# One maximum instruction for a tile's two heads, and a newly planned order of all steps

## The chip, the cores and the metric

The kernel runs on one core of a Trainium2 chip. The metric is the device time of one execution in microseconds (us). A profile of one further execution was taken by the hardware profiler; the times of single instructions come from it.

## What is computed

Rotary attention followed by a two-layer MLP. q, k and v are float32 arrays of 4 batches, 8 heads, 576 positions and 64 channels.

```python
q_rot, k_rot = (rotate(q), rotate(k))           # by cos and sin of position x frequency
scores = scale * np.matmul(q_rot, k_rot.transpose(0, 1, 3, 2))
scores = scores - np.max(scores, axis=-1, keepdims=True)
attn = np.exp(scores)
attn = attn / (np.sum(attn, axis=-1, keepdims=True) + 1e-09)
attn_out = np.matmul(attn, v)
x = attn_out.transpose(0, 2, 1, 3).reshape(2304, 512)
h = x @ w_in                                    # 512 x 2048
g = np.where(h >= 1, h, np.where(h <= -1, 0.0, (h + 1) ** 2 / 4))
out = g @ w_out                                 # 2048 x 512
```

## The kernel before

**Numbers.** Each float32 operand of a matmul is cut into two 16-bit halves, a high and a low one, and a product is three matmuls (high by high, high by low, low by high; `TERMS`, L601). ACT writes a high half, DVE the low half (`split`, L348). The weights arrive as 64-bit words, are put together from them by three DVE instructions (L506, L508, L510) and are cut in 16 chunks (`prep_w`, L494); for the first ten of them PE and ACT make the low half (L535 to L539), for the rest DVE (L527).

**Attention.** A tile is 128 positions of q for a pair of heads. There are 4 batches x 4 pairs x 4 tiles = 64 of them. `scores` (L573) is one step of 12 matmuls on PE; it fills two PSUM tiles `psS`, one for each head, of two banks each; only the first 576 columns are used. Then `softmax_item` (L548): for each head DVE takes the negative maximum of a row into `mx` (L556), ACT makes the exp with that as its bias and sums the row (L558); ACT scales the sums of both (L561), DVE inverts them (L563), ACT writes each head's high half into `phl` (L566) and DVE its low half (L568). A transpose by the DMA, issued on SP's queue, turns `phl` into `pT` (L300). After two tiles of the same pair of heads comes the step of values, 28 matmuls on PE (`pv_group`, L613, with L611). It uses v in `vS` and copies of it at shifted positions in `vM`, which are written by DMAs on SP's queue (L296, in `prep_v`). The last 64 positions of a batch are left over: for each pair of heads one such tile holds the 64 positions of both heads in its 128 rows, and its softmax has one head's worth of instructions (`attention_left`, L659, with `scores_left`, L588; it uses one of the two `psS` tiles in turn). So there are 2 x 64 + 16 = 144 maxima.

**MLP.** A block of 256 rows of x runs through 8 steps. In each, two groups of 12 matmuls fill `psH` (L692), ACT and DVE form g and its low half (L699 to L713), and two groups of 6 matmuls add to two banks `psO` (L722). ACT writes the result (L732) and SP stores it.

**The order.** Nothing is issued while it is described. Every step is put into a `Plan` (L72) with its engine, its cost in ns, its due time `at`, and what it reads and writes. `wanted` (L113) works out a rank for each step, back from the PE steps in order of `at`; `order` (L132) adds the offsets of the table `SLACK` (L25, in ns, by group and engine and sometimes by part; larger is later) and then simulates five in-order queues, PE, ACT, DVE and the DMA issuers SP and POOL, taking on each the ready step of lowest rank. The steps whose group is `init`, `first` or `raw w` are taken first wherever they are ready. What comes out is the order in which each engine's instructions stand on the chip. The groups have names: `s0` is the softmax of batch 0 and `s1` that of the later batches, `w` the cutting of weights, `k1` the preparing of K for a later batch, `pv` the values, `mlp0` to `mlp3` the blocks of the MLP, and `first` the loads of K, Q and V of batch 0. The costs in question: 760 ns for a scores step (L585), `pe_cost(14, n + 58) + 130` for a values step (L614), which is 2003 ns for n = 256 with `pe_cost` of L279, and for a DMA its bytes at 400 GB/s (L296). `dve_cost` (L285) stands 665 ns for a maximum of 576 columns.

Of the kernel before, what the change touches and what calls it, by code (L numbers as in the profile page):

```python
# [25 lines left out]
    "k0.03 dve": -18_500, "k1 act": 68_700, "k1 dve": 128_000, "k1.12 dve": 2_700, "k1.20 dve": 192_800,  # L26
    "k1.22 act": -86_400, "k1.30 dve": -49_500, "k1.32 act": 53_100, "k1.32 dve": -154_900, "left0 act": 751_500,
    "left0 dve": -109_200, "left0.02 act": -54_200, "left0.03 dve": 207_500, "left1 act": 1_401_000,
    "left1 dve": 2_700, "left1.11 pe": -109_700, "left1.12 act": 41_400, "left1.13 dve": -9_600,
    "left1.30 dve": -29_400, "left1.32 dve": -130_500, "left1.33 pe": 94_600, "mlp0 act": -95_500,  # L30
    "mlp0 dve": -1_118_000, "mlp0 pe": 285_700, "mlp0.0.1 pe": 49_700, "mlp0.0.6 act": -53_100,
    "mlp1 pe": -97_500, "mlp1.1.1 dve": 59_700, "mlp1.1.2 dve": 25_400, "mlp1.1.3 act": 26_000,
    "mlp1.1.5 act": 26_200, "mlp2 act": -133_700, "mlp2 pe": -214_800, "mlp2.2.0 pe": 14_800,
    "mlp2.2.3 act": 167_900, "mlp2.2.3 dve": -287_900, "mlp2.2.3 pe": 44_800, "mlp2.2.7 pe": 97_000,
    "mlp3 act": 8_500, "mlp3 dve": -2_019_800, "mlp3 pe": 139_200, "mlp3.3.0 pe": -130_200,
    "mlp3.3.2 pe": -19_100, "mlp3.3.3 act": -53_700, "mlp3.3.3 pe": -76_300, "mlp3.3.5 act": -184_500,
# [12 lines left out]
    "s0.032 pe": -138_600, "s1 act": 10_000, "s1 dve": 6_000, "s1 pe": -526_500, "s1.100 dve": 8_000,
# [147 lines left out]
def kernel(  # L197
# [12 lines left out]
    nc = tc.nc  # L210
# [12 lines left out]
    def sbt(name, shape, dt=F32):  # L223
        return sb.tile(shape, dt, name=name)
# [661 lines left out]
```

## Time and profile before

| what | value |
|---|---|
| median of 3 runs | 636.36 us (635.49 to 637.52) |
| the profiled execution, its own time | 633.81 us |
| its span, from the first to the last instruction | 632.0 us |
| mean granted TensorE clock | 0.98 of full speed |
| PE busy | 559.8 us, 5078 matmuls |
| DVE busy | 511.2 us, 839 instructions |
| ACT busy | 441.0 us, 881 instructions |
| data moved by the DMA engines | 91.33 MB |

How to read it: PE is TensorE's matmul engine, DVE VectorE, ACT ScalarE, SP and POOL issue DMAs. Each engine works its own queue in order, so an instruction that waits holds up all behind it on that engine. The recorded duration of an instruction on DVE or ACT overlaps the start of the next one a little; the distance from start to start is what it costs the engine. A busy share over the whole span is an average over stages with different limits.

### The profile page before, as it was taken

The page shows a single profiled execution, that of the slowest core. Times are in us where ns is not written, and L with a number is a line of the kernel's source. Part 1 is how long each engine was busy: PE and PEld are TensorE (multiplying, and loading weights), DVE is VectorE, ACT ScalarE, POOL GpSimd, SP SyncE. Part 2 cuts the span into 40 slices and gives each one's busy share as a digit, 9 for nine tenths or more (in the row PEclk, how much of TensorE's full clock was granted, in tenths as well). Part 3 has the DMA queues.
Part 4 walks back from the last instruction along what each step waited for, and adds up shares of the span by engine and source line. Part 5 has one row for each costly group of instructions (what it writes and reads, how often), then busy time and mean ns, then how long its engine had stood idle before and what let it go on. Part 6 is the DMA issues. An engine that isn't in the chain of part 4 may idle for free.

```text
span 632.0 us, 12652 instructions
## 1 busy us (share of the span) xinstructions
PE 559.8 (89%) x5078; PEld 358.6 (57%) x5078; DVE 511.2 (81%) x839; ACT 441.0 (70%) x881; POOL 7.5 (1%) x18
## 2 busy tenths in 40 slices
PE   1346678799997999999998999999999999999995
PEld 1112234566654666666665676676666676666663
DVE  5998999999999999998897889889877874333422
ACT  3647898978999799984878798877787663232221
POOL 0000100000000000000000000000000000000000
PEclk9997879999998999999999999999999999999999
DMA  8997988695699858876377765856666553000000
GB/s 265 372 305 261 258 231 161 133 233 132 142 260 203 195 99 188 205 164 161 92 163 129 124 127 109 136 94 115 113 131 129 85 99 77 1 8 27 1 34 18
DMA packets 188011, 91.33 MB, mean 145 GB/s; under 512 B 170160, under 2 KB 178608, under 8 KB 185904
## 3 DMA queue, kind: packets, MB, share of 16 engines
q1 hardware_dynamic: 186224, 77.94, 56.0%
q0 software_dynamic: 1728, 12.58, 5.6%
q8 instruction: 40, 0.66, 0.4%
q14 instruction: 19, 0.16, 0.1%
HBM read 40.96 MB, written 4.72 MB: 72 GB/s over the span
## 4 chain that ended last, share of the span: by engine, by line
PE 56%; DVE 22%; DMA 12%; ACT 6%; issue 3%; SPq 0%; ACTq 0%
PE psO L722 21%; PE psH L692 21%; PE psV L611 7%; PE psS L582 5%; DMA pT<-phl 5%; DVE phl L568 4%; DVE mx L556 3%; DMA rk<-in_km_dram 3%; DMA vM<-vS 2%; ACT p L558 2%; DVE g L713 1%; ACT phl L566 1%; DMA rv<-in_vm_dram 1%; DVE r L709 1%; DVE xT L508 1%
## 5 line engine op out<-in xcount | busy, mean ns | idle before, releaser
L722 PE MATMUL psO<-w,g 128*128 128x512 f16 x864 | 211.7, 380 | 1.9 <-ACT g L711 0.9
L692 PEld LDWEIGHTS <-w 128*128 128x128 f16 x1920 | 170.9, 98 | 44.4 <-issue 5.2
L692 PE MATMUL psH<-xT,w 128*128 128x256 f16 x1536 | 187.7, 273 | 3.2 <-ACT a L699 3.2
L558 ACT ACTIVATE p<-psS,mx 128x576 f32<-128x576 f32 x144 | 105.3, 733 | 26.1 <-DVE mx L556 20.1
L722 PEld LDWEIGHTS <-g 128*128 128x128 f16 x864 | 79.3, 98 | 75.2 <-DVE g L713 2.5
L568 DVE SCALAR_TENSOR_TENSOR phl<-p,sums,phl 128x576 f16<-128x576 f32 x144 | 113.4, 812 | 9.6 <-ACT phl L566 9.6
L566 ACT ACTIVATE phl<-p,sums 128x576 f16<-128x576 f32 x144 | 105.0, 765 | 17.5 <-DVE sums L563 15.2
L556 DVE TENSOR_REDUCE mx<-psS 128x1 f32<-128x576 f32 x144 | 104.3, 750 | 6.9 <-PE psS L582 6.2
L582 PE MATMUL psS<-kT,qT 64*128 64x512 f16 (+1 forms) x768 | 64.5, 295 | 22.6 <-ACT p L558 15.3
L711 ACT ACTIVATE g<-r 128x512 f16<-128x512 f32 x72 | 44.9, 624 | 47.5 <-DVE r L709 29.2
L699 ACT ACTIVATE a<-psH 128x512 f32<-128x512 f32 x72 | 42.4, 590 | 49.3 <-PE psH L692 48.7
L713 DVE SCALAR_TENSOR_TENSOR g<-r,g 128x512 f16<-128x512 f32 x72 | 49.5, 688 | 26.8 <-ACT g L711 26.7
L582 PEld LDWEIGHTS <-qT 64*128 64x128 f16 x768 | 31.2, 97 | 68.5 <-issue 47.9
L702 DVE SCALAR_TENSOR_TENSOR r<-a 128x512 f32<-128x512 f32 x48 | 33.1, 689 | 45.6 <-ACT a L699 45.2
L611 PE MATMUL psV<-pT,vS 128*64 128x256 f16 (+1 forms) x768 | 50.1, 253 | 3.8 <-DMA pT<-phl 3.5
L709 DVE SCALAR_TENSOR_TENSOR r<-a,r 128x512 f32<-128x512 f32 x72 | 49.6, 689 | 0.9
L611 PEld LDWEIGHTS <-vS 128*64 128x64 f16 x768 | 33.3, 112 | 18.5 <-issue 14.7
L611 PE MATMUL psV<-pT,vM 128*64 128x256 f16 (+1 forms) x480 | 29.2, 253 | 3.3 <-DMA vM<-vS 3.3
L558 ACT ACTIVATION_READ_ACCUMULATOR p<-psS,mx 128x1 f32 x144 | 28.1, 195 | 0.0
L692 PE MATMUL psH<-xL,w 128*128 128x128 f16 x384 | 25.5, 219 | 0.0
L611 PEld LDWEIGHTS <-vM 128*64 128x64 f16 x480 | 22.0, 113 | 4.1 <-DMA vM<-vS 3.8
L535 PE MATMUL psO<-xT,xL 128*128 128x512 f32 x20 | 15.4, 864 | 9.8 <-DVE xT L510 5.6
(98 smaller groups left out, 467.5 us busy)
## 6 DMA issues: line engine op xcount, KB each, us to landing
w<-in_w_in_dram POOLq DMA_DIRECT2D x5, 1024.0 KB, 6.9
rv<-in_vm_dram SPq DMA_DIRECT2D x8, 512.0 KB, 5.7
w<-in_w_out_dram POOLq DMA_DIRECT2D x4, 1024.0 KB, 7.3
out_dram<-o SPq DMA_DIRECT2D x16, 256.0 KB, 2.4
rq<-in_qm_dram SPq DMA_DIRECT2D x7, 512.0 KB, 7.2
dup<-in_qm_dram SPq DMA_DIRECT2D x7, 512.0 KB, 3.9
dup<-in_km_dram SPq DMA_DIRECT2D x6, 576.0 KB, 5.3
rk<-in_km_dram SPq DMA_DIRECT2D x6, 576.0 KB, 6.8
```

What stands on the lines that cost most here:

```text
L556: plan.add("dve", dve_cost(S, psum=True), at, lambda m=m, src=src: nc.vector.tensor_reduce(out=m, in_=src, op=ALU.max, axis=AX.X, negate=T ...
L558: plan.add("act", act_cost(S, psum=True, ptrs=2), at, lambda a=a, e=e, m=m, src=src: nc.scalar.activation(out=p32[e], in_=src, func=AF.Exp ...
L566: plan.add("act", act_cost(S), at, lambda a=a, e=e, hi=hi: nc.scalar.activation(out=hi, in_=p32[e], func=AF.Copy, scale=rr[:, a:a + 1]), r ...
L568: plan.add("dve", dve_cost(S, ptrs=1), at, lambda a=a, e=e, hi=hi, lo=lo: nc.vector.scalar_tensor_tensor(out=lo, in0=p32[e], scalar=rr[:, ...
L582: nc.tensor.matmul(out=psS[a][:, lo:hi], lhsT=qT[hf][d, l, j, c:c + 128], rhs=kT[ks][d, j, m, lo:hi], start=z == 0, stop=z == 2)
L611: nc.tensor.matmul(out=outs[a], lhsT=st, rhs=moving(a, blk), start=z == 0, stop=z == len(seq) - 1)
L692: nc.tensor.matmul(out=psH[:, n * i:n * i + n], lhsT=wi[ft // 2][:, wl, kk, 128 * (ft % 2):128 * (ft % 2) + 128], rhs=xfn(xl, kk), start=z ...
L699: plan.add("act", act_cost(512, psum=True, ptrs=0), at, lambda one=one: nc.scalar.activation(out=a, in_=psH, func=AF.Relu, scale=2.0 ** -7 ...
L709: plan.add("dve", dve_cost(512), at, lambda one=one: nc.vector.scalar_tensor_tensor(out=r, in0=a, scalar=one, in1=r, op0=ALU.max, op1=ALU. ...
L711: plan.add("act", act_cost(512, ptrs=0), at, lambda g=g, one=one: nc.scalar.activation(out=g[:, 0], in_=r, func=AF.Relu, scale=1.0, bias=- ...
L713: plan.add("dve", dve_cost(512), at, lambda g=g, one=one: nc.vector.scalar_tensor_tensor(out=g[:, 1], in0=r, scalar=-one, in1=g[:, 0], op0 ...
L722: nc.tensor.matmul(out=psO[pos[tt]], lhsT=g[:, gl, n * i + 128 * tt:n * i + 128 * tt + 128], rhs=wo[ft // 2][:, wl, ft % 2, :], start=ft = ...
```

## The change

Four things are changed.

- The maxima. For a tile of two heads there is one reduction, which reads 2 x 576 columns and writes two columns of `mx`; both exps now depend on it. For this the two `psS` tiles are halves of one PSUM tile and the two `mx` tiles are two columns of one. Left-over tiles keep their reduction of 576 columns.
- Costs of PE steps in the plan: a scores step 930 ns instead of 760, a values step `pe_cost(14, n) + 200`, which is 1735 ns for n = 256.
- Rates of loads in the plan: in the groups `init` and `first` 320 GB/s instead of 400, for v 250 and for the rotation table 220.
- The table `SLACK` is replaced as a whole. Some of the offsets in ns, old to new: `s0 dve` -17,100 to -149,000, `w dve` 26,100 to 31,300, `s0 act` -202,700 to -31,300, `w act` -133,500 to 158,600, `k1 dve` 128,000 to 48,000, `pv0 pe` -206,300 to -429,100, `mlp0 pe` 285,700 to -189,900. The rest of the planner is as it was.

```diff
@@ -260,10 +253,11 @@
     idn = xL_w[:, 0:256].bitcast(F32)
     ndg = [xL_w[:, 256 + 128 * i:384 + 128 * i].bitcast(BF16) for i in range(2)]
     xL_keys = [("xL", l, e) for l in range(2) for e in range(2)]
-    mx = [[sbt(f"mx{i}_{a}", [128, 1]) for a in range(2)] for i in range(4)]
+    mx = [sbt(f"mx{i}", [128, 2]) for i in range(4)]
     sums = [sbt(f"sums{i}", [128, 4]) for i in range(4)]
 
-    psS = [ps.tile([128, 1024], F32, name=f"psS{i}") for i in range(2)]
+    psS_t = ps.tile([128, 2048], F32, name="psS")
+    psS = [psS_t[:, 1024 * i:1024 * i + 1024] for i in range(2)]
     psV = ps.tile([128, 512], F32, name="psV")
     psH = ps.tile([128, 512], F32, name="psH")
     psO = [ps.tile([128, 512], F32, name=f"psO{i}") for i in range(2)]
@@ -291,9 +285,9 @@
         nsca[0] += 1
         return sca[:, nsca[0] - 1:nsca[0]], ("sca", nsca[0])
 
-    def dma(at, dst, src, r, w, nbytes, eng="sp", chain=[]):
+    def dma(at, dst, src, r, w, nbytes, eng="sp", chain=[], rate=320.0):
         q = nc.sync if eng == "sp" else nc.gpsimd
-        plan.add(eng, 600.0 if eng == "sp" else 1000.0, at, lambda: q.dma_start(out=dst, in_=src), r, w + chain, bw=nbytes / 400.0)
+        plan.add(eng, 600.0 if eng == "sp" else 1000.0, at, lambda: q.dma_start(out=dst, in_=src), r, w + chain, bw=nbytes / (rate if plan.group in ("init", "first") else 400.0))
 
     def dmaT(at, dst, src, r, w, nbytes):
         plan.add("sp", nbytes / 221.0 + 60.0, at,
@@ -444,7 +438,7 @@
     def load_v(b, at):
         plan.group, plan.part = "raw v1" if b else "first", b
         for hf in range(2):
-            dma(at, rv[:, 2 * hf:2 * hf + 2], vm[b][:, 2 * hf:2 * hf + 2], [], [("rv", hf)], 128 * 4096)
+            dma(at, rv[:, 2 * hf:2 * hf + 2], vm[b][:, 2 * hf:2 * hf + 2], [], [("rv", hf)], 128 * 4096, rate=250.0)
         dma(at, rvL, vl[b], [], ["rvL"], 64 * 2048)
 
     vfac = {}
@@ -551,13 +545,15 @@
         sm, rr = sums[ri][:, 0:nh], sums[ri][:, 2:2 + nh]
         sk = [("sums", ri, a) for a in range(nh)]
         es = [ring("p32", 3) for _ in range(nh)]
+        srcs = psS_t.rearrange("p (a s) -> p a s", a=2)[:, :, 0:S] if nh == 2 else psS[slot][:, 0:S]
+        plan.add("dve", dve_cost(nh * S, psum=True), at, lambda: nc.vector.tensor_reduce(
+            out=mx[ri][:, 0:nh], in_=srcs, op=ALU.max, axis=AX.X, negate=True),
+            r=[("psS", slot + a) for a in range(nh)], w=[("mx", ri)])
         for a, e in enumerate(es):
-            m, src = mx[ri][a], psS[slot + a][:, 0:S]
-            plan.add("dve", dve_cost(S, psum=True), at, lambda m=m, src=src: nc.vector.tensor_reduce(
-                out=m, in_=src, op=ALU.max, axis=AX.X, negate=True), r=[("psS", slot + a)], w=[("mx", ri, a)])
+            m, src = mx[ri][:, a:a + 1], psS[slot + a][:, 0:S]
             plan.add("act", act_cost(S, psum=True, ptrs=2), at, lambda a=a, e=e, m=m, src=src: nc.scalar.activation(
                 out=p32[e], in_=src, func=AF.Exp, bias=m, accum_out=sm[:, a:a + 1]),
-                r=[("psS", slot + a), ("mx", ri, a)], w=[("p32", e), sk[a]])
+                r=[("psS", slot + a), ("mx", ri)], w=[("p32", e), sk[a]])
         plan.add("act", 188.0, at, lambda: nc.scalar.activation(
             out=sm, in_=sm, func=AF.Copy, scale=2.0 ** -14, bias=1e-9 * 2.0 ** -14), r=sk, w=sk)
         plan.add("dve", 81.0, at, lambda: nc.vector.reciprocal(out=rr, in_=sm), r=sk, w=[("sums", ri, 2)])
@@ -582,7 +578,7 @@
                         nc.tensor.matmul(out=psS[a][:, lo:hi], lhsT=qT[hf][d, l, j, c:c + 128],
                                          rhs=kT[ks][d, j, m, lo:hi], start=z == 0, stop=z == 2)
 
-        plan.add("pe", 760.0, at, mm, r=[("qT", hf, j, x) for x in range(2)] + [("kT", ks, j, x) for x in range(2)],
+        plan.add("pe", 930.0, at, mm, r=[("qT", hf, j, x) for x in range(2)] + [("kT", ks, j, x) for x in range(2)],
                  w=[("psS", 0), ("psS", 1)])
 
     def scores_left(at, b, j):
@@ -611,7 +607,7 @@
                 nc.tensor.matmul(out=outs[a], lhsT=st, rhs=moving(a, blk), start=z == 0, stop=z == len(seq) - 1)
 
     def pv_group(at, j, slot, n, c0, pkeys):
-        plan.add("pe", pe_cost(14, n + 58) + 130, at, lambda: values(
+        plan.add("pe", pe_cost(14, n) + 200, at, lambda: values(
             [psV[64 * a:64 * a + 64, c0:c0 + n] for a in range(2)], lambda a, i: pT[slot][:, 9 * a + i, 0:n], j),
             r=vkeys + pkeys, w=["psV"])
 
@@ -740,7 +736,7 @@
     def left_rows(b0):
         return lambda i: [(slice(64 * e, 64 * e + 64), out[(b0 + e) * S + SM:(b0 + e + 1) * S, :]) for e in range(2)]
 
-    dma(-20, rt, rot, [], ["rt"], 128 * 2 * 4 * S)
+    dma(-20, rt, rot, [], ["rt"], 128 * 2 * 4 * S, rate=220.0)
 
     def init():
         make_identity(nc, idn)
```

## Rows read from the trace of the kernel before

**Rows 1.** The page's busy times: busy us, share of the span, instructions.
```profile
PE 559.8 (89%) x5078; PEld 358.6 (57%) x5078; DVE 511.2 (81%) x839; ACT 441.0 (70%) x881; POOL 7.5 (1%) x18
```

**Rows 2.** Busy us by stretch: PE, PEld, DVE, ACT, POOL, clock, DMA share, GB/s.
```profile
0.00:120.00 120.00, 65.13 (x389) 33.21 (x390) 108.12 (x201) 85.31 (x169) 5.41 (x14) 0.93 0.86 250
120.00:340.00 220.00, 209.21 (x1957) 135.07 (x1957) 209.77 (x322) 187.34 (x375) 2.10 (x4) 0.98 0.75 172
340.00:632.00 292.00, 285.44 (x2738) 190.36 (x2734) 193.31 (x318) 168.32 (x338) 0.00 (x0) 1.00 0.42 81
```

**Rows 3.** PE's waits from 340 us: us in total, times, longest.
```profile
PE psO L722 <- ACT g L711: 0.9, 1, 0.9
```

**Rows 4.** The page's chain that ended last: shares by engine and by line.
```profile
PE 56%; DVE 22%; DMA 12%; ACT 6%; issue 3%; SPq 0%; ACTq 0%
PE psO L722 21%; PE psH L692 21%; PE psV L611 7%; PE psS L582 5%; DMA pT<-phl 5%; DVE phl L568 4%; DVE mx L556 3%; DMA rk<-in_km_dram 3%; DMA vM<-vS 2%; ACT p L558 2%; DVE g L713 1%; ACT phl L566 1%; DMA rv<-in_vm_dram 1%; DVE r L709 1%; DVE xT L508 1%
```

**Rows 5.** PE's waits between 120 and 340 us.
```profile
PE psV L611 <- DMA vM<-vS: 3.3, 2, 1.7
PE psS L582 <- ACT p L558: 3.0, 5, 1.1
```

**Rows 6.** DVE in order of time: start us, us, instruction.
```profile
111.29 1.42 DVE L556 TENSOR_REDUCE mx<-psS 128x1 f32<-128x576 f32 x2
112.62 0.69 DVE L506 TENSOR_SCALAR o<-w 128x1024 uint32<-128x1024 uint32 x1
...
117.54 1.54 DVE L568 SCALAR_TENSOR_TENSOR phl<-p,sums,phl 128x576 f16<-128x576 f32 x2
...
134.33 0.15 DVE L316 TENSOR_REDUCE sca<-psV 128x1 f32<-128x4 f32 x1
134.40 0.80 DVE L568 SCALAR_TENSOR_TENSOR phl<-p,sums,phl 128x576 f16<-128x576 f32 x1
```

**Rows 7.** Instructions of L556 before 340 us, of L594 between 120 and 340.
```profile
L556 DVE TENSOR_REDUCE mx<-psS x82: 727/749/764, 17.7 to 333.8; 128x1 f32<-128x576 f32 x82
...
L594 PE MATMUL psS<-kT,qL x48: 192/284/380, 152.6 to 301.8; 128*128 128x512 f16 x24, 128*128 128x64 f16 x24
```

**Rows 8.** ACT in order of time, the exps of the pair in rows 6.
```profile
112.08 0.74 ACT L558 ACTIVATE p<-psS,mx 128x576 f32<-128x576 f32 x1 [0.19 <-DVE mx L556]
...
112.81 0.73 ACT L558 ACTIVATE p<-psS,mx 128x576 f32<-128x576 f32 x1
```

**Rows 9.** PE's waits before 120 us.
```profile
PE psS L582 <- ACT p L558: 12.3, 7, 4.6
```

**Rows 10.** PE in order of time: a values step (28 matmuls), a scores step.
```profile
103.87 0.63 PE L611 MATMUL psV<-pT,vS 128*64 128x256 f16 x8 [0.70 <-DMA pT<-phl]
...
105.52 1.13 PE L535 MATMUL psO<-o,xL 128*128 128x512 f32 x2
...
107.87 0.91 PE L582 MATMUL psS<-kT,qT 64*128 64x512 f16 x12
108.71 2.79 PE L692 MATMUL psH<-xT,w 128*128 128x256 f16 x24
```

**Rows 11.** Stretches as in rows 2, for loads and for the clock.
```profile
0.00:16.00 16.00, 2.50 (x10) 2.13 (x12) 9.27 (x38) 5.85 (x12) 0.69 (x6) 1.00 0.84 264
16.00:60.00 44.00, 18.50 (x71) 7.73 (x68) 39.82 (x78) 27.12 (x55) 1.72 (x3) 0.93 0.96 313
...
200.00:220.00 20.00, 18.45 (x156) 11.19 (x156) 18.47 (x31) 16.20 (x35) 0.00 (x0) 0.83 0.91 197
```

**Rows 12.** DVE in order of time, near 50 us: K of batch 1.
```profile
50.47 1.36 DVE L341 TENSOR_TENSOR rk<-rk,rt 128x1152 f32<-128x1152 f32 x1 [2.60 <-DMA rk<-in_km_dram]
```

**Rows 13.** PE in order of time, 202 to 208 us.
```profile
202.13 1.28 PE L611 MATMUL psV<-pT,vM 128*64 128x256 f16 x10 [1.55 <-DMA vM<-vS]
...
204.40 1.62 PE L582 MATMUL psS<-kT,qT 64*128 64x512 f16 x12
205.96 2.12 PE L692 MATMUL psH<-xT,w 128*128 128x256 f16 x12
```

More of the change, by code (lines that the diff above doesn't have):

```diff
@@ L31 @@
[L31 to L36, printed above, removed]
@@ L58 @@
-    "scale1 act": 46_200, "scale1 dve": -64_900, "v0.0 dve": 57_600, "v1 dve": -37_900, "v1 pe": 90_800,
-    "v1 sp": 248_200, "v1.3 pe": 30_000, "w act": -133_500, "w dve": 26_100, "w.0 dve": 8_200, "w.1 act": 319_600,
-    "w.1 dve": -38_900, "w.2 dve": -35_200, "w.3 act": 1_600, "w.3 dve": 60_900, "w.4 pe": -9_100,
-    "w.5 dve": 83_100,
+    "k0 dve": -184_300, "k1 act": -183_400, "k1 dve": 48_000, "k1.10 dve": 23_700, "k1.12 dve": 19_000,
+    "k1.20 dve": 419_800, "k1.22 act": 131_300, "k1.22 dve": 125_500, "k1.30 dve": 78_100, "left0 dve": -126_200,
@@ new lines @@
+    "left0.00 dve": 96_100, "left0.02 dve": -122_900, "left0.03 pe": -107_800, "left1 act": -530_400,
+    "left1 dve": -548_300, "left1 pe": -3_900, "left1.11 pe": 43_100, "left1.21 pe": -63_900, "mlp0 act": 4_100,
+    "mlp0 dve": -117_900, "mlp0 pe": -189_900, "mlp0.0.2 dve": 198_600, "mlp0.0.4 pe": 120_900,
+    "mlp0.0.5 act": 33_700, "mlp0.0.6 dve": -16_300, "mlp0.0.7 pe": -72_700, "mlp1 act": -2_900,
+    "mlp1 pe": 50_700, "mlp1.1.2 pe": 17_600, "mlp1.1.4 act": -25_200, "mlp1.1.5 dve": -61_200,
@@ new lines @@
+    "mlp1.1.6 pe": -21_100, "mlp2 act": -246_200, "mlp2 pe": 20_300, "mlp2.2.2 pe": 260_200,
+    "mlp2.2.3 pe": -60_600, "mlp2.2.5 pe": 20_700, "mlp2.2.7 pe": -161_300, "mlp3 act": -1_320_400,
+    "mlp3 dve": -64_400, "mlp3 pe": 91_900, "mlp3.3.0 pe": 486_600, "mlp3.3.3 pe": 224_500,
+    "mlp3.3.6 dve": 74_600, "mlp3.3.6 pe": -62_300, "mlp3.3.7 pe": -19_300, "mlp3.4.0 pe": 55_500,
+    "mlp3.4.1 pe": -389_700, "mlp3.4.3 pe": -7_800, "mlp3.5.0 pe": 61_600, "mlp3.5.1 act": -102_900,
+    "mlp3.5.4 pe": 51_600, "mlp3.5.6 pe": 40_900, "mlp3.5.7 act": 9_200, "mlp3.5.7 pe": -241_300,
@@ new lines @@
+    "mlp3.6.2 pe": -95_900, "mlp3.6.3 pe": -34_400, "mlp3.7.0 pe": -247_100, "mlp3.7.1 pe": 27_900,
+    "pv0 dve": 84_200, "pv0 pe": -429_100, "pv0.001 dve": -10_500, "pv0.003 dve": 17_400, "pv1 dve": -129_900,
+    "pv1 pe": -44_500, "pv1.320 pe": -401_000, "pv1.321 dve": 80_600, "q0 dve": 22_300, "q0.000 dve": 34_500,
+    "q0.001 dve": -65_900, "q0.002 dve": -187_800, "q0.003 dve": -102_100, "q0.010 dve": 19_400,
+    "q0.013 dve": 37_200, "q1 dve": 134_400, "q1.100 dve": -55_500, "q1.210 dve": 259_500, "q1.300 dve": -128_000,
@@ new lines @@
+    "ql0.0 dve": -49_100, "ql1 dve": 39_900, "raw q0.0 sp": -65_400, "raw q1 sp": 27_800, "raw q1.210 sp": 11_400,
+    "s0 act": -31_300, "s0 dve": -149_000, "s0 pe": -142_200, "s0.000 dve": -44_700, "s0.001 dve": 15_800,
+    "s0.002 dve": 14_400, "s0.021 dve": 1_800, "s0.023 act": 25_900, "s0.032 dve": 43_000, "s1 act": 1_500,
+    "s1 dve": -35_100, "s1 pe": -119_700, "s1.100 act": 13_100, "s1.100 dve": -272_800, "s1.101 act": -7_100,
+    "s1.101 pe": 7_200, "s1.103 dve": 89_000, "s1.111 act": 49_900, "s1.112 act": -22_800, "s1.113 dve": 63_000,
@@ new lines @@
+    "s1.120 act": -49_700, "s1.122 act": 146_200, "s1.131 act": -38_400, "s1.201 act": -81_700,
+    "s1.201 dve": -123_800, "s1.210 dve": -31_700, "s1.211 dve": 35_400, "s1.220 dve": -23_200,
+    "s1.310 dve": -191_300, "s1.311 dve": 2_100, "s1.323 dve": -30_600, "s1.330 dve": -117_100,
+    "s1.333 act": -14_300, "scale1.20 dve": -78_500, "v0 act": 141_300, "v0 dve": 10_400, "v0.0 dve": 50_400,
+    "w act": 158_600, "w dve": 31_300, "w.2 act": -88_800, "w.4 dve": -45_900, "w.5 dve": 59_900,
@@ L62 @@
+    "w.7 dve": 5_900,
 }
```

26 lines of the change are left out of this document (removed).

## The prediction, written before the changed kernel ran

> **What bounds the kernel now.** I start with the page's busy shares: PE is busy 559.8 us of a span of 632.0 and DVE 511.2 [rows 1]. Averages over such a span hide stages, so next come the busy times of three stretches [rows 2]. From 340 us on PE is busy 285.4 of 292 us, with one wait of 0.9 us [rows 3]; the rest is the tail behind its last matmul. There DVE is busy only 193.3 us and no rearrangement of DVE work is worth anything. From 120 to 340 us both are nearly full: PE 209.2 and DVE 209.8 of 220. In the first 120 us DVE is busy 108.1 us and PE only 65.1. So PE's idle time is 54.9 us before 120, 10.8 us between 120 and 340 and 6.6 us behind, 72.2 us together, and a faster kernel has to take its gain out of the first two. The chain that ended last says the same: the four largest PE lines hold 54% of it and DVE 22% [rows 4], which is 139 us, and since PE never starves behind 340 us I put that share into the first 340 us: 139/340 = 0.41. That fraction is how I price DVE time saved there. Which waits end last on PE between 120 and 340 us is in [rows 5]: a load of shifted values 3.3 us, the exp that frees the score banks 3.0 us in five places. The time compared is the profiled execution's 633.81 us (span plus 1.8); the median of the runs is 636.36, 2.55 above it, and I carry each difference over to that median.
>
> **Part 1, one maximum for two heads: DVE time.** 64 tiles of two heads now need 64 reductions where there were 128; the 16 left-over tiles of one head keep theirs, so DVE runs 64 instructions fewer. Two back to back take 1.33 us from the start of the first to the next instruction (111.29 to 112.62), one alone takes half, 0.67 [rows 6]. The merged size is in no row. Its elements cost what the present ones cost: the smallest reduction, 4 elements from PSUM, hands DVE on after 0.07 us (134.33 to 134.40) [rows 6], so 572 more elements cost 0.60 us, 1.04 ns each, and 1152 elements 0.07 + 1148 x 0.00104 = 1.265 us. That saves 0.065 us a pair. The bounds are 1.20 us (no fixed part at all) and 1.33 us (crossing from one head's banks to the other's costs a second fixed part); I take 1.265, since it rests on two sizes of the same operation. Before 340 us there are 82 reductions [rows 7]; 8 of them belong to left-over tiles (48 matmuls of L594, six a tile) [rows 7], so 37 pairs: 37 x 0.065 = 2.4 us of DVE, and by the share of 0.41, **1.0 us** of the end (bounds 0 and 4.8, the second for 1.20 us with all of it on the chain). The 27 pairs behind 340 us lie beside a full PE and give nothing.
>
> The Trainium skill, Perfetto Trace Analysis, section Optimizing Scalar/DVE Operations, puts the fixed part of a DVE operation on PSUM at about 125 ns of engine time and advises grouping where the engine is saturated. By that figure the estimate would be 37 x 0.125 = 4.6 us of DVE and 1.9 us of the end. Here the trace disagrees with its 0.07 us, and the sum stays with the trace.
>
> **Part 2, the first exp starts later.** Today ACT's first exp begins at 112.08, 0.79 us after the pair of maxima began, and the second follows 0.73 us later, at 112.81 [rows 8]: the second maximum is hidden under the first exp. Merged, the first exp waits for both: 1.265 - 0.67 = 0.60 us later, and the second with it, and the score banks and the row sums come free 0.60 us later. Who waits behind it: ACT's queue, and the next scores on PE, for which PE stood in line 7 times before 120 us [rows 9] and 5 times after [rows 5]. Before 120 us the delay costs nothing as long as DVE has other work in its queue, and it has (108 of 120 us, start included). After that, 5 x 0.60 = 3.0 us; half of it should be met by planning those scores later, so **+1.5 us** (bounds 0, and 12 x 0.60 = 7.2).
>
> **Part 3, the steps planned anew.** Every step's place may change, so no row prices it directly. I ask whether the planner's new figures lie nearer to the trace and which known mistakes cost time. A values step has 1.65 us on PE (103.87 to 105.52); the old figure works out at 2.00, the new at 1.735. A scores step has 0.84 us (107.87 to 108.71) [rows 10]; 0.76 before, 0.93 now, as wrong as it was but on the safe side, since at the lower clock it takes 1.62 [rows 13]. The first loads were planned at 400 GB/s, and the chip moved 264 in the first 16 us and 313 in the next 44 [rows 11]; 320, 250 and 220 are nearer. So of the three kinds of figures two are much better. What the old figures cost: at 50.47 DVE had stood 2.60 us, in order, behind K of batch 1 [rows 12], data that no tile of batch 0 needs, with weights waiting to be cut. A plan that knows the loads to be late would not put that step there; the chain passes this wait, and I take half, **1.3 us**. Between 120 and 340 us PE idles 10.8 us. At 200 to 220 us the granted clock averages 0.83 [rows 11], so about a third of those 20 us ran at 1.2 instead of 2.4 GHz, 0.17 x 20 = 3.4 us of lost work, right after the 1.55 us wait for shifted values: twelve scores matmuls took 1.62 us and twelve of L692 2.12 [rows 13], where 24 of them take 2.79 at the full clock [rows 10]. Of 10.8 + 3.4 = 14.2 us a better-informed order should save some, but it brings waits of its own; I take a third, **4.7 us** (bounds 14.2 gained, and 7 lost, from the second rival). SP's queue goes with it: its transposes and reloads keep their count and sizes and only change places, priced in the same third. Nothing is added to PE, ACT or DMA; the score tile and the maxima only become parts of one tile each.
>
> Sum: -1.0 + 1.5 - 1.3 - 4.7 = -5.5 us: 628.3 for the profiled execution, **630.9 us** for the median. A measurement of this kernel can tell about 0.3% (1.9 us) from no change.
>
> **Rival 1: the waits only move.** DVE and PE are both about 95% busy between 120 and 340 us, so little is free, and a shorter wait in one place can return in the next. Then parts 1 to 3 come to -1.0 + 1.5 and noise: 634.5 to 638.2 us. For it speaks that PE and DVE are so evenly full; against it the 54.9 us before 120.
>
> **Rival 2, slower: weights come too late.** The offsets put the softmax of batch 0 ahead of the weight cutting by far more than before on DVE (s0 minus w: from -43 to -180 us) and on ACT (from -69 to -190). PE's feed is the MLP, whose first matmul starts at 108.71 [rows 10], after 10 pairs of maxima. If all 16 tiles of batch 0 went first, DVE would spend 6 x 2.87 us (1.33 for the maxima, 1.54 for the two low halves [rows 6]) = 17 us more before it, and PE would get 6 x 0.84 + 3 x 1.65 = 10 us of work for it: 7 us lost, 643 us, range 640 to 646. It decides if the first matmul of L692 moves beyond about 118 us. Against it: DVE fills gaps between softmax steps, which wait for scores and exp, with weights anyhow.
>
> **Rival 3, slower: the longer hold of the score banks.** If all 12 waits of part 2 grow by 0.60 us and PE has nothing else in line, that is 7.2 - 1.0 = +6.2 us: 642.6, range 638.5 to 643. Against it: five of the twelve only lie where PE is nearly full. Beside it stands the same section of the Trainium skill, by which breaking instructions up may complete work sooner where DVE is not saturated but causes bubbles elsewhere; no run here shows that yet. It is the case in which the order would be innocent and the merged instruction guilty. A variant in which the joined score tile makes left-over tiles wait for each other's banks is worth at most 8 x 1.5 us before 340 us, and I give it 0.02.
>
> **How the numbers follow.** Forecast (faster by over 1.9 us) 0.58; rival 1 0.19; rivals 2 and 3 0.12 and 0.09, with the variant 0.23 on the slower side. The forecast's own range is 622 to 634.4: the lower end takes 14.2 us, all idle and slow-clock time of the middle. The range of 622 to 641 leaves out some 0.08 below (if the start also shortens by several us) and 0.11 above, most of rivals 2 and 3.
>
> **What would show it.** The reduction: 64 of 128x2 from 128x1152 at about 1.35 us each, with 1.26 to the next start. Part 2: exp's wait for the maxima longer by 0.6 us a place. Part 3: no wait for batch 1's K on DVE near 50 us, PE's idle time between 120 and 340 us below 8 us, no stretch there at a lower clock. I am wrong if PE's idle time in the first 120 us grows beyond 55 us, or the first L692 matmul comes much later than 109 us, or PE shows new gaps behind 340 us.

## The result, and the profile after

The changed kernel takes 642.78 us (median of 20 runs, 634.79 to 648.77), the kernel before 635.21 us beside it (631.69 to 639.41, 20 runs): ratio 1.0072, 95% interval 1.0045 to 1.0098. It is **slower**, where 630.9 us and "faster" were forecast, and outside the range of 622 to 641. The ratio leaves out executions more than 1.5% above the fastest of their kernel, here eight of the 20 of after, the profiled one (646.93 us, span 644.7) among them, and none of before, so the medians lie further apart than it says, 7.6 us. A second profile of the same kernel (e1 below, 643.88 us) shows the same stall, though a shorter one. The lines of after are numbered anew: the maxima are L549, exp L554, the low halves phl L562 (ScalarE, here ACT) and L564 (VectorE, DVE), scores L578, values L607, the MLP's first product L688 (L692 before), loads L290, transposes L294.

I read the stretches first (columns as in [rows 2]; the last is the stretch around the stall). Busy times, after:

```profile
0.00:120.00 120.00, 58.06 (x324) 29.43 (x325) 99.60 (x177) 75.83 (x150) 5.05 (x14) 0.84 0.97 245
120.00:340.00 220.00, 207.68 (x1953) 135.99 (x1950) 210.44 (x300) 188.28 (x376) 2.11 (x4) 0.99 0.75 169
340.00:644.70 304.70, 294.51 (x2810) 194.86 (x2804) 197.96 (x299) 175.33 (x357) 0.00 (x0) 1.00 0.42 81
52.00:68.00 16.00, 6.14 (x19) 2.67 (x19) 8.05 (x11) 8.05 (x15) 0.53 (x1) 0.50 1.06 195
```

PE idles 61.9 us before 120 (54.9 before), 12.3 between 120 and 340 (10.8) and 10.2 behind (6.6), 84.4 us where there were 72.2; with 0.5 us more busy time that is the whole 12.7 us of span. Most of the loss stands in the first 120 us. PE's waits there, after:

```profile
PE psS L578 <- ACT p L554: 24.8, 6, 12.8
PE psV L305 <- ACT w L299: 10.3, 2, 7.5
PE psV L305 <- DVE sca L322: 8.7, 1, 8.7
```

One wait for the score banks alone is 12.8 us long, where seven together were 12.3 [rows 9]. Who made exp late is one step further back: the longest waits of PE, ACT and DVE between 50 and 64 us, after:

```profile
PE psS L578 <- ACT p L554: 12.8, 1, 12.8
ACT phl L562 <- DMA pT<-phl: 9.1, 1, 9.1
DVE phl L564 <- ACT phl L562: 8.2, 1, 8.2
```

ACT could not write the next high half, because the transposes that read the buffer had not ended; exp stood behind it in ACT's queue, and DVE and PE behind exp. The SP queue in order of time (start, time on SP's queue, which is not the time to landing; x2 runs from the start of the first to the end of the second), after:

```profile
22.91 5.66 SPq L290 DMA_DIRECT2D rk<-in_km_dram  x1
28.67 0.38 SPq L290 DMA_DIRECT2D dup<-in_km_dram  x1
29.14 0.51 SPq L290 DMA_DIRECT2D rk<-in_km_dram  x1
29.74 0.55 SPq L290 DMA_DIRECT2D rq<-in_qm_dram  x1
32.98 24.92 SPq L294 DMA_TRANSPOSE pT<-phl  x2
```

and in the kernel before:

```profile
27.23 1.24 SPq L296 DMA_DIRECT2D dup<-in_km_dram  x1
28.57 10.91 SPq L300 DMA_TRANSPOSE pT<-phl  x2
39.57 1.01 SPq L296 DMA_DIRECT2D rk<-in_km_dram  x2
```

The first of these transposes alone, from issue to landing, after and then before:

```profile
DMA to landing us min/median/max: 25.0/25.0/25.0
```
```profile
DMA to landing us min/median/max: 10.1/10.1/10.1
```

The first two transposes of batch 0 held SP's queue for 24.92 us instead of 10.91: the new plan issues four loads for batch 1, 2.3 MB, just ahead of them, three of which stood behind them before. Two loads of weights on POOL's queue came earlier too, at 31.8 and 37.1 us instead of 39.2 and 40.3, and so moved beside the transposes. PE waited so long that the granted clock was 0.50 from 52 to 68 us, the lower of its two levels, 1.2 GHz. The wait for K of batch 1 on DVE [rows 12] is gone; this one took its place. The MLP began late, after:

```profile
118.20 1.03 PE L688 MATMUL psH<-xT,w 128*128 128x256 f16 x4
```

against 108.71 [rows 10]. The merged reduction itself, after (count, ns min/median/max, first and last start; then DVE in order of time):

```profile
L549 DVE TENSOR_REDUCE mx<-psS x80: 747/1349/1358, 26.8 to 526.7; 128x2 f32<-128x1152 f32 x64, 128x1 f32<-128x576 f32 x16
```
```profile
125.16 1.35 DVE L549 TENSOR_REDUCE mx<-psS 128x2 f32<-128x1152 f32 x1
126.42 0.81 DVE L564 SCALAR_TENSOR_TENSOR phl<-p,sums,phl 128x576 f16<-128x576 f32 x1
```

It is 1.35 us long and hands DVE on after 1.26; two reductions took 1.33 before.

### The profile page after: what moved, and what is told of

It reads as the page before. It is cut to its first block, busy times and chain, and to the rows that moved or that the text cites. A ratio compares the mean times of both kernels' runs of the same rounds, so it can differ in the third digit from the quotient of the medians.

```text
span 644.7 us, 12575 instructions
## 1 busy us (share of the span) xinstructions
PE 560.3 (87%) x5078; PEld 360.3 (56%) x5078; DVE 508.0 (79%) x775; ACT 439.4 (68%) x881; POOL 7.2 (1%) x18
## 4 chain that ended last, share of the span: by engine, by line
PE 47%; DVE 18%; DMA 14%; issue 14%; ACT 5%; SPq 1%; POOL 0%; ACTq 0%; POOLq 0%; DVEq 0%
PE psO L718 18%; PE psH L688 18%; DMA pT<-phl 6%; PE psV L607 5%; DVE phl L564 4%; PE psS L578 4%; DVE mx L549 3%; DMA rk<-in_km_dram 2%; ACT p L554 1%; DMA w<-in_w_out_dram 1%; DMA rv<-in_w_out_dram 1%; DVE r L705 1%; DVE dup L337 1%; ACT phl L562 1%; DMA rv<-in_vm_dram 1%
## 5 line engine op out<-in xcount | busy, mean ns | idle before, releaser
L688 PEld LDWEIGHTS <-w 128*128 128x128 f16 x1920 | 171.6, 98 | 50.0 <-issue 9.5
L688 PE MATMUL psH<-xT,w 128*128 128x256 f16 x1536 | 189.8, 275 | 6.7 <-ACT a L695 6.7
L554 ACT ACTIVATE p<-psS,mx 128x576 f32<-128x576 f32 x144 | 105.1, 733 | 35.0 <-DVE mx L549 27.8
L564 DVE SCALAR_TENSOR_TENSOR phl<-p,sums,phl 128x576 f16<-128x576 f32 x144 | 112.6, 810 | 14.2 <-ACT phl L562 14.2
L562 ACT ACTIVATE phl<-p,sums 128x576 f16<-128x576 f32 x144 | 104.5, 766 | 26.2 <-DVE sums L559 13.4
L549 DVE TENSOR_REDUCE mx<-psS 128x2 f32<-128x1152 f32 (+1 forms) x80 | 98.2, 1230 | 12.0 <-PE psS L578 8.1
L578 PE MATMUL psS<-kT,qT 64*128 64x512 f16 (+1 forms) x768 | 64.6, 304 | 27.0 <-ACT p L554 25.3
L578 PEld LDWEIGHTS <-qT 64*128 64x128 f16 x768 | 31.3, 99 | 72.2 <-issue 44.2
L607 PE MATMUL psV<-pT,vS 128*64 128x256 f16 (+1 forms) x768 | 50.7, 256 | 7.4 <-DMA pT<-phl 7.4
L607 PEld LDWEIGHTS <-vS 128*64 128x64 f16 x768 | 33.7, 112 | 21.9 <-issue 11.9
L607 PE MATMUL psV<-pT,vM 128*64 128x256 f16 (+1 forms) x480 | 29.3, 253 | 1.9 <-DMA vM<-vS 1.9
L554 ACT ACTIVATION_READ_ACCUMULATOR p<-psS,mx 128x1 f32 x144 | 28.2, 196 | 0.0
L688 PE MATMUL psH<-xL,w 128*128 128x128 f16 x384 | 26.2, 219 | 0.0
L607 PEld LDWEIGHTS <-vM 128*64 128x64 f16 x480 | 22.2, 114 | 2.5 <-DMA vM<-vS 2.1
L305 PE MATMUL psV<-ssk,ones 128*128 128x1 f32 (+1 forms) x14 | 3.2, 298 | 19.7 <-ACT w L299 10.3
```

Source lines behind the costliest of these rows:

```text
L549: plan.add("dve", dve_cost(nh * S, psum=True), at, lambda: nc.vector.tensor_reduce(out=mx[ri][:, 0:nh], in_=srcs, op=ALU.max, axis=AX.X, n ...
L554: plan.add("act", act_cost(S, psum=True, ptrs=2), at, lambda a=a, e=e, m=m, src=src: nc.scalar.activation(out=p32[e], in_=src, func=AF.Exp ...
L562: plan.add("act", act_cost(S), at, lambda a=a, e=e, hi=hi: nc.scalar.activation(out=hi, in_=p32[e], func=AF.Copy, scale=rr[:, a:a + 1]), r ...
L564: plan.add("dve", dve_cost(S, ptrs=1), at, lambda a=a, e=e, hi=hi, lo=lo: nc.vector.scalar_tensor_tensor(out=lo, in0=p32[e], scalar=rr[:, ...
L578: nc.tensor.matmul(out=psS[a][:, lo:hi], lhsT=qT[hf][d, l, j, c:c + 128], rhs=kT[ks][d, j, m, lo:hi], start=z == 0, stop=z == 2)
L607: nc.tensor.matmul(out=outs[a], lhsT=st, rhs=moving(a, blk), start=z == 0, stop=z == len(seq) - 1)
```

## The experiments

Two theories stood at the start. **Loads**: the new order's loads ahead of the first transposes cost the time. **Hold**: the merged reduction does, since the first exp waits for both heads and the score banks are held longer (the prediction's rival 3). Where steps are moved, the planner's list of steps is edited just before it is issued, so that line numbers shift by some; each kernel ran in five rounds beside the kernel before.

**e1, the changed kernel again**, no edit.

> The changed kernel as it is, for a second trace and as the base of the others. In its first trace the first two transposes of softmax results were issued at 33 us and landed 25 us later, behind 2.3 MB of loads for batch 1 that SP had issued just before and 2.1 MB of weights that POOL issued at 31.8 and 37.1; DVE stood 8.2 us behind it, PE 12.8. Theory A (transposes queue behind loads): the same stall again, of varying length, since how the queues share the DMA engines varies; time 635 to 649, median about 643, and its length explains a good part of each execution's time. Theory B (the merged maximum): the stall is a side matter, the time is 640 to 645 whatever its length.

Measured: 640.45 us (637.99 to 654.77, 7 runs), ratio 1.0085 [1.0049, 1.0122]. The SP queue of this run:

```profile
32.80 21.14 SPq L294 DMA_TRANSPOSE pT<-phl  x2
```

The first transpose landed after 21.2 us: the stall is there again, 3.8 us shorter, and so is a wide spread of the times. PE idles 57.9, 14.4 and 8.4 us by stretch here, so of this run's loss less than half lies before 120 us.

**e2, the new order with two maxima.**

```diff
+        def maxima():
+            for a in range(nh):
+                nc.vector.tensor_reduce(out=mx[ri][:, a:a + 1], in_=psS[slot + a][:, 0:S], op=ALU.max, axis=AX.X, negate=True)
-        plan.add("dve", dve_cost(nh * S, psum=True), at, lambda: nc.vector.tensor_reduce(
...
+        plan.add("dve", dve_cost(nh * S, psum=True), at, maxima,
```

> The changed kernel with its order kept instruction for instruction, except that in the place of each merged maximum stand two of 576 columns, so that the first exp may start after the first. Theory A: the maxima are worth little: between -3 and +3 us against the changed kernel (DVE loses 64 x 0.06 = 4 us over the whole span, the exps gain 0.6 us where they are waited for). Theory B: 5 to 8 us faster than the changed kernel, back to about 636.

Measured: 645.03 us (641.29 to 652.61, 6 runs), ratio 1.0136 [1.0106, 1.0166]. Undoing the merge in the new order gains nothing (4.6 us over e1 by the medians, outside the ranges of both theories): the order alone is slow.

**e3, SP's four loads behind the first two transposes**, still merged.

```diff
+        moved = [nth(*x) for x in [('raw k1.10 sp', 0), ('raw k1.10 sp', 1), ('raw k1.12 sp', 0), ('raw q1.100 sp', 0)]]
+        goal = nth(*('s0.010 sp', 0))
...
+        out = [i for i in out if i not in moved]
+        at = out.index(goal) + 1
+        out[at:at] = moved
```

> The changed kernel, with four loads for batch 1 on SP's queue (three of K, one of q, 2.3 MB, some 5.7 us at 400 GB/s) moved behind the first two transposes; nothing else moves on any engine. Theory A: the transposes land some 6 us earlier, DVE's stall near 50 us falls from 8.2 to about 2 us, and the time by 4 to 7 us, to 636 to 639. Theory B: no change beyond 1.5 us.

Measured: 638.15 us, ratio 1.0049 [1.0029, 1.0069], and all 11 runs between 636.64 and 640.38. The first transpose landed after 13.4 us. The interval overlaps those of after and e1, so what this move is worth by itself is not clear of noise. The spread is 3.7 us, for 14.0 in the 20 runs of after; but e4 and e8 below, with the same loads moved, spread over 9.6 and 10.8 us, so that the spread goes with the stall is not shown. 3.4 us are still lost, and DVE of this run shows a new wait:

```profile
54.49 1.36 DVE L350 TENSOR_TENSOR rk<-rk,rt 128x1152 f32<-128x1152 f32 x1 [4.80 <-DMA rk<-in_km_dram]
```

**e4, POOL's first two weight loads late as well**, held by a copy on POOL that reads the transposed data.

```diff
+                nc.gpsimd.tensor_copy(out=gate, in_=pT[0][:, 0, 128:129])
+                load()
```

> As the third, and POOL's first two weight loads (2.1 MB) wait in addition until the second transpose has landed (a copy of one column on POOL reads what it wrote). Theory A: the two transposes take about 11 us as in the kernel before, no stall of DVE near 50 us, and 6 to 9 us off the time of the changed kernel, 634 to 637, with a spread as small as that of the kernel before (some 6 us); if the weights now come too late, a new wait of DVE for them near 60 us gives up to 5 us back. Theory B: no change or slower.

Measured: 638.64 us (636.21 to 645.82, 11 runs), ratio 1.0055 [1.0027, 1.0083]: no better than e3 and not the 634 to 637 hoped for, although the first transpose now landed after 4.8 us. With SP's loads out of the way POOL's cost no time; what they cost beside SP's loads no run shows, for none moves them alone.

**e5, the old order with the merged maximum**, issued where the first of the two stood.

```diff
+            def maxima(done=done, srcs=srcs):
+                if not done:
+                    nc.vector.tensor_reduce(out=mx[ri][:, 0:nh], in_=srcs, op=ALU.max, axis=AX.X, negate=True)
+                    done.append(1)
```

> The kernel before, its order kept, with one merged maximum in the place of the first of each tile's two. Theory B (the merged maximum costs: the first exp starts 0.6 us later) : 2 to 6 us slower than the kernel before. Theory C, formed after the second experiment, where two maxima in the changed order were slower than the merged one by about 0.5%: the merged instruction is a gain by itself, and the loss lies in the new order alone: 1 to 4 us faster than the kernel before, 631 to 634.

Measured: 644.13 us (642.22 to 649.49, 6 runs), ratio 1.0155 [1.0113, 1.0197], before 634.48. The merge alone, which saves DVE time, costs 9.7 us in the old order. Where PE stood in line from 340 us on, in this kernel:

```profile
PE psS L590 <- ACT p L566: 2.7, 4, 0.9
PE psS L602 <- ACT p L566: 2.4, 3, 1.3
PE psO L730 <- ACT g L719: 0.9, 1, 0.9
```

Only the last of them was there before [rows 3]. The stretch behind 340 us, in this kernel:

```profile
340.00:642.90 302.90, 290.05 (x2775) 192.96 (x2773) 195.90 (x296) 171.93 (x350) 0.00 (x0) 1.00 0.42 79
```

PE idles 12.9 us there, 6.6 before. Over the whole span PE waits for score banks 25.9 us here (14.4, 5.7 and 5.8 by stretch, the two waits for the maxima of L562 counted), 15.3 before [rows 5, 9].

**e6, V of batch 0 earlier in the new order; e7, that and the late loads of e4.** A third theory: the first values step came at 87.5 us, 60.9 before, since V was cut late.

```diff
+        for goal, moved in [(318, [95, 96, 98, 99, 100, 101, 102, 103]), (319, [104, 105, 106]), (330, [308]), (343, [344]), (354, [355, 331])]:
+            out = [i for i in out if i not in moved]
+            out[out.index(goal) + 1:out.index(goal) + 1] = moved
```

> The changed kernel with the cutting of V of batch 0 (3 instructions on ACT, 3 large ones on DVE, 3 copies by DMA) moved forward to just behind the softmax of the third tile, the first two values steps moved forward behind it, and the transposes of the third pair issued as soon as their softmax is there. Theory D (V late): in the new order the first values step comes at 80 to 87 us (60.9 before); until it has freed its buffer the third pair's transposes can't start, so four of them run in a row from 82 to 104 us at 5.3 us each, where the plan counts 2.7, and the first MLP matmul waits for the last (110 to 118 us, 108.7 before). Then here the first values step comes 15 us earlier, the first MLP matmul 4 to 10 us earlier than in the changed kernel (113 to 118), and the time falls by 3 to 8 us to 633 to 638. If V's lateness is covered by the weights, which also have to be cut before the MLP, the first MLP matmul moves by under 2 us and the time by under 1.5 us.

> The changed kernel with both repairs: the loads on SP and POOL behind the first two transposes as in the fourth experiment, and V early as in the sixth. Theories A and D together: no stall near 50 us and the first MLP matmul before 108 us; 630 to 634, as fast as or faster than the kernel before. If the loss lies elsewhere (in the middle and late stretches, where PE idled 2 and 2 us more than before): 636 to 638.

Measured: 640.91 us (640.12 to 649.77, 6 runs) and 639.54 (637.52 to 644.63, 12 runs), first values at 69.1 and 64.2 us. Nothing over e1 and e4, and e7 misses both of its ranges: the late V is no cause.

**e8, e3 with two maxima** (the edits of e3 and e2 together).

> The new order with the four loads of SP behind the first two transposes (as in e3, 638.15 us), and two reductions over 576 columns in place of each merged one, both still issued where the merged one is. Theory (the merged reduction costs by making the first exponential late): the first exponential can start after the first of the two, 0.6 us earlier in each of 64 pairs, so banks and buffers come free earlier and the time falls to 632 to 636.5. Rival (in an order planned for it the merged reduction costs nothing): the kernel is as fast as e3 or slower by the 64 x 0.07 us more of VectorE, 638 to 642.

Measured: 639.34 us (634.86 to 645.63, 10 runs), ratio 1.0092 [1.0059, 1.0125]. The rival holds: in the new order the merge costs nothing.

**e10 and e11, why the merge costs in the old order.** Both keep two reductions and two separate score tiles, and issue both where the first stood; only the order of the two differs.

```diff
+            def maxima(done=done):
+                for c in () if done else (1, 0)[-nh:]:
+                    nc.vector.tensor_reduce(out=mx[ri][c], in_=psS[slot + c][:, 0:S], op=ALU.max, axis=AX.X, negate=True)
+                done.append(1)
```

> The order of before, two reductions, two separate score tiles; both reductions are issued where the first was, that of head 1 ahead of that of head 0. Nothing is merged and VectorE saves nothing: the first exponential alone comes later, by one reduction (0.6 us or more), as with the merged one. Theory (the later first exponential holds the score banks longer): as slow as the merged reduction in the order of before, 641 to 647. Rival (what cost there was the single score tile, or the long instruction itself): 634 to 637.

> As the reversed kernel, but head 0 is reduced first, so that its exponential can start as early as before; only the second reduction is issued earlier than it was, ahead of the VectorE work that stood between the two. Theory (later first exponential): the same as before within 0.3 per cent, 633.5 to 637, and 6 or more us below the reversed kernel. Rival (VectorE work pushed behind the second reduction is what costs): 640 to 646, like the reversed kernel.

Measured on one chip: **645.34 us** reversed (643.18 to 648.42, 6 runs; ratio 1.0199 [1.0153, 1.0246]) and **635.70 us** in natural order (633.64 to 637.92, 12 runs; 1.0043 [1.0016, 1.007]). DVE does the same work at the same places; 9.6 us hang on whether the first exp must wait for the second reduction. The page's costliest groups (busy, mean ns, idle before), the exps, reversed and then natural:

```profile
L564 ACT ACTIVATE p<-psS,mx 128x576 f32<-128x576 f32 x144 | 105.6, 735 | 42.8 <-DVE mx L560 35.7
```
```profile
L564 ACT ACTIVATE p<-psS,mx 128x576 f32<-128x576 f32 x144 | 105.2, 732 | 23.2 <-DVE mx L560 14.0
```

ACT waits 35.7 us for maxima instead of 14.0. In one pair, ACT in order of time, reversed and then natural:

```profile
113.68 0.74 ACT L564 ACTIVATE p<-psS,mx 128x576 f32<-128x576 f32 x1 [0.73 <-DVE mx L560]
```
```profile
112.15 0.74 ACT L564 ACTIVATE p<-psS,mx 128x576 f32<-128x576 f32 x1 [0.20 <-DVE mx L560]
```

The maxima of that pair began at 112.17 and 111.36: exp follows 1.51 and 0.79 us later. Neither the longer instruction nor the joined tile is needed for the loss. The natural order is itself 0.4% slower than before, where the same within 0.3% was expected: issuing the second reduction early may cost something of its own. How the delay becomes 9.6 us the traces show only in part. Before 120 us and over the whole span, reversed and then natural:

```profile
0.00:120.00 120.00, 66.86 (x378) 33.63 (x379) 107.12 (x199) 83.90 (x165) 5.42 (x14) 0.90 0.85 250
0.00:641.10 641.10, 566.31 (x5078) 361.78 (x5078) 513.65 (x839) 440.32 (x881) 7.52 (x18) 0.98 0.61 142
```
```profile
0.00:120.00 120.00, 63.69 (x389) 32.29 (x390) 107.77 (x201) 84.79 (x169) 5.74 (x14) 0.93 0.87 250
0.00:633.10 633.10, 559.25 (x5078) 358.34 (x5078) 511.76 (x839) 440.25 (x881) 7.84 (x18) 0.98 0.62 144
```

PE's idle time differs by 0.9 us only (74.8 and 73.9); it is 4.3 us longer behind 340 us and 3.2 us shorter before 120. The rest is PE's busy time, 7.1 us more for the same matmuls, at a granted clock of 0.90 instead of 0.93 before 120 us; how much of it the clock explains, no run separates.

**e9, the old order with one DVE step moved**: the pass over K of batch 1 that waits 2.60 us [rows 12] goes behind the second values copy.

```diff
+        for goal, moved in [(101, [476])]:
+            out = [i for i in out if i not in moved]
+            out[out.index(goal) + 1:out.index(goal) + 1] = moved
```

> The order of before and its two reductions, with one VectorE step alone moved: the first pass over K of batch 1 (rk<-rk,rt, which began at 50.47 us after 2.60 us of waiting for its load) behind the second values copy, some 15 us later. Theory (VectorE is what bounds the first 120 us, so that wait is on the path): up to 2.6 us off, 632 to 634.5. Rival (waits only move: the first transposes and the weights set the stretch): no change, 634.5 to 636.

Measured: 632.02 us (629.93 to 634.26, 12 runs), ratio 0.9975 [0.9948, 1.0002]: at the edge, so it ran again as e15.

**e12, the new order with both repairs**: e3's loads behind the transposes, and the DVE pass that then waited 4.80 us for one of them moved too. **e13** is the same with two maxima.

```diff
+        for goal, moved in [(307, [466, 467, 472, 488]), (101, [474])]:
+            out = [i for i in out if i not in moved]
+            out[out.index(goal) + 1:out.index(goal) + 1] = moved
```

> The new order and the merged reduction, with two repairs at once: the four loads of SP behind the first two transposes (as in e3, 638.15 us), and the first VectorE pass over K of batch 1, which in e3 began at 54.49 us after 4.80 us of waiting for one of those loads, moved behind the second values copy. Theory (what e3 still loses to before is that wait, which the moved loads only handed from the transposes to VectorE): up to 4.8 us off e3, 633.5 to 636. Rival (the new order is slower for other reasons: the long exponentials' chain, the late weights): no change, 637 to 639.5.

> The kernel of e12 with two reductions over 576 columns in place of each merged one, issued where the merged one is. Theory (merging costs only where the order was planned for two reductions): the same as e12 within 2 us. Rival (with the load waits gone the later first exponential shows here too): 2 to 6 us below e12.

Measured: 635.94 us (631.76 to 637.35, 12 runs), ratio **1.0013 [0.999, 1.0036]**, and 636.66 (633.37 to 642.97, 12 runs), 1.0027 [0.9998, 1.0056]. Five steps moved, and the new order is as fast as the old one; merged or not makes no difference to it that these runs resolve. The stretches of e12:

```profile
0.00:120.00 120.00, 68.85 (x429) 36.54 (x430) 109.93 (x196) 86.61 (x172) 5.05 (x14) 0.90 0.91 254
120.00:340.00 220.00, 206.72 (x1920) 134.14 (x1919) 205.22 (x290) 186.17 (x373) 2.10 (x4) 0.98 0.75 172
340.00:634.50 294.50, 286.41 (x2734) 189.78 (x2730) 192.40 (x290) 167.29 (x338) 0.00 (x0) 1.00 0.42 79
```

PE idles 51.2, 13.3 and 8.1 us, 72.5 together; before 72.2, in after 84.4, in e1 80.7 and in e3 79.5. So in the traces the move of the loads alone took 1.2 to 4.9 us off PE's idle time, both moves together 8.2 to 11.9. The first MLP matmul is at 107.0 us, in e3 at 113.3.

**e14, the old order with all three DVE passes over that K moved**, and what hangs on them. **e15, e9 again.**

```diff
+        for goal, moved in [(397, [476, 477, 478, 479, 497])]:
```

> The order of before and its two reductions, with the three VectorE passes over K of batch 1's first half (4.1 us), the ScalarE sum of squares behind them and the one load that waits for it moved behind the second VectorE step of the first block of the multilayer part, some 20 to 60 us later. Theory (VectorE bounds the stretch up to the first block, which needs the weights that VectorE splits): the 2.6 us of e9 and part of the 2.7 us of the two later passes, 629 to 632. Rival (PE waits there for exponentials and loads): as e9, 631.5 to 634.5; should the later chain make the next batch's K late, slower than before.

> The kernel of e9 once more, on the chip of the three others: its ratio was 0.9975 with an interval that just reached 1. If the wait taken out is real the ratio is 0.995 to 0.999 again, 631 to 633.5 us; if e9 was chance it lies at 1.000 to 1.002.

Measured: e14 639.77 us (635.91 to 644.97, 11 runs), ratio 1.0076 [1.0048, 1.0104]; e15 **631.35 us** (629.11 to 635.87, 9 runs) against 634.17, ratio **0.9955 [0.9926, 0.9984]**, faster than both kernels. The stretches of e14 and then of e15:

```profile
0.00:120.00 120.00, 69.01 (x413) 35.50 (x414) 108.21 (x201) 83.99 (x165) 6.39 (x14) 0.94 0.87 245
120.00:340.00 220.00, 204.27 (x1883) 131.08 (x1882) 205.87 (x315) 182.63 (x364) 2.10 (x4) 0.98 0.74 172
```
```profile
0.00:120.00 120.00, 67.28 (x392) 34.22 (x393) 108.74 (x201) 85.66 (x170) 5.41 (x14) 0.93 0.86 250
120.00:340.00 220.00, 209.74 (x1963) 135.14 (x1962) 210.19 (x324) 187.34 (x376) 2.10 (x4) 0.99 0.75 173
```

In e14 the MLP begins at 104.8 us and PE is 3.9 us busier before 120 than in the kernel before, as hoped; between 120 and 340 it loses 4.9. Its waits there, in e14:

```profile
PE psH L700 <- ACT a L707: 6.4, 4, 4.6
PE psS L590 <- ACT p L566: 3.2, 4, 1.3
PE psV L319 <- ACT dup L404: 3.0, 1, 3.0
```

The last is the sum of squares behind the moved passes, now late itself. In e15 only the step that waited moves, and PE is 2.2 us busier before 120 and 0.5 between 120 and 340.

## Why the prediction was wrong

All three signs named for being wrong came: 61.9 us of PE idle before 120, the MLP at 118.2, new gaps behind 340.

**What bounds the kernel**: right that the order gains or loses mostly in the first 340 us; wrong that behind 340 us "no rearrangement of DVE work is worth anything". DVE has time to spare there, but what it delivers late still holds others up: with the merge in the old order PE waits there again for exps and maxima that had never held it up (e5: 12.9 us idle behind 340, where the kernel before has 6.6).

**Part 1**: right in size (1.26 us to the next start, 1.265 forecast). Whether its 1.0 us of the end came, the runs can't tell: in the new order the merged kernel has the lower ratio in each of three pairs (e1 and e2, e3 and e8, e12 and e13, by 0.0051, 0.0043 and 0.0014), but the intervals of each pair overlap.

**Part 2**: +1.5 us was not what made this kernel slow, for the three pairs show no cost of the delay in the new order; the old order pays 9.7 us (e5) and, with the delay alone, 9.6 (e10 against e11), more than the bound of 7.2. I took the five waits behind 120 us, halved, with DVE's full queue as cover before 120 us, and all twelve as the bound. The delay makes new waits: ACT waited for maxima in 24 places before, 43 in e10. The small variant with the joined tile exists as well, left-over scores that wait 4.2 us in e5 (L602) and 0.8 in e10, but e10 is as slow without it. The Trainium skill, Perfetto Trace Analysis, section Optimizing Scalar/DVE Operations, says that breaking up instructions of an engine that is not saturated, but causes bubbles on others, may let work complete sooner. Behind 340 us the traces agree: there DVE is busy 195.9 of 302.9 us in e5, and one instruction in the place of two leaves PE idle 12.9 us instead of 6.6. By the same section of the Trainium skill grouping can improve throughput where the engine is saturated; no run here shows such a gain clear of noise.

**Part 3 is the step that failed**: -6.0 us were forecast for the new order, -1.3 and -4.7, where the changed kernel lost 7.6 by the medians, and undoing the merge gave nothing back (e2). The half that I took of 2.60 us and the third of 14.2 stand in for an order I could not see: the 4.7 us were to come from 120 to 340 us, where PE idled 12.3 us instead of 10.8, and 13.3 even in e12. The 2.60 us wait was real and on the path: with it removed e9 and e15 gain 2.4 and 2.8 us by the medians, only e15 clear of noise. But the new plan got rid of it by issuing the loads ahead of the transposes, and the sentence that SP's transposes and reloads "only change places, priced in the same third" is what broke: after that change of place the first transpose landed after 25.0 us instead of 10.1, and PE waited 12.8 us. Moving the four loads back, and with them the DVE step that would then wait, takes the loss away (e12, whose interval lies below those of after and e1). The planner's code charges each of the two 2.73 us of SP and at most 2.67 more for what lies ahead on the wire, 10.8 us for both, and the queue held them 10.9 to 24.9; that it chose the order for this reason is argued, not shown. The new loading rates do not touch that figure.

**Rivals.** Rival 2 gave 640 to 646 us if the first MLP matmul moved beyond 118 us, and rival 3 gave 642.6; it came at 118.2 in after, and 642.78 us fits both. Both fit by luck. Rival 2's cause was not it: e12 leaves the planned order of softmax and weights as it is, and with its five other steps moved the matmul comes at 107.0, earlier than in the kernel before (113.2 in e1, 113.3 in e3). Rival 3's mechanism is real in the old order, but its line "the order would be innocent" does not hold: the new order hides this delay (e2, e8, e13) and loses by its own doing. Rival 1, waits that only move, is what e3 and e14 show in small: 4.8 us handed from the transposes to DVE, 3.9 us gained and 4.9 given back.

Still open: why the new order hides the later exp. It was planned with it, but no run isolates which steps give the cover. Open too is the part of POOL's loads in the stall (last section). Each trace is one execution, and the stall varies from one to the next.

## What to carry to other kernels

Before merging two instructions, ask what the first result was good for by itself: a saving of 0.07 us a pair on a busy engine cost 9.7 us in an order made for two, because its consumer had started on the first half. When a plan moves loads, look at what else their queue carries, above all transposes that read a buffer others wait for, and at what moves beside it on other queues. Where a step stands at the head of an in-order engine and waits, try moving that step alone: here that gained 2.8 us (e15), and moving what follows it as well lost 5.6 (e14).

## What the hardware showed unexpectedly

Transposes of the same size land after very different times. The first of batch 0 took 10.1 us from issue to landing before, 20.9 to 25.0 in the four profiles with the loads ahead of it (after, e1, e2, e6), 9.4 to 13.4 with SP's loads behind it (e3, e8, e12, e13), and 4.8 and 4.7 with POOL's two loads behind it as well (e4, e7). The 25.0 us of after fall into stretches; the DMA packets from 34 to 44, from 46 to 56.6 and from 56.6 to 60 us, and the second load of POOL (issued at 37.14; its size, and us to landing):

```profile
DMA packets 1147, 3.77 MB, mean 377 GB/s; under 512 B 208, under 2 KB 597, under 8 KB 922
DMA packets 973, 0.49 MB, mean 46 GB/s; under 512 B 943, under 2 KB 943, under 8 KB 943
DMA packets 3245, 0.89 MB, mean 263 GB/s; under 512 B 3201, under 2 KB 3201, under 8 KB 3245
w<-in_w_out_dram POOLq DMA_DIRECT2D x1, 1024.0 KB, 19.5
```

Nearly all packets of the last two stretches, in which the transposes ran, are under 512 bytes. Until 44 us hardly any of these pass, while the loads move at 377 GB/s. Then they pass slowly, 943 in 10.6 us, and from 56.6 us on fast, 3201 in 3.4 us; at 56.7 us POOL's load lands. In e1 the rate jumps at 52.5 us, from 794 packets in 6.5 us to 3352 in 3.5, and there POOL's load lands at 52.5. So the size of the packets alone does not make them slow. That they were slow because of POOL's unfinished load is argued from this coincidence, not shown.
